# Channel-major and token-major operands, four 64x64 array tiles and 768-column weight blocks in an attention, MoE and MLP kernel

## The chip, the core and the metric

The kernel runs on one core of a Trainium2 chip. Five engines work side by side, each through its own queue in order: PE (the matmul array; PEld is its weight load), DVE (VectorE), ACT (ScalarE), POOL (GpSimd) and SP, which here issues DMAs. SBUF is the working memory, PSUM holds what PE writes. The metric is the device time of one execution in microseconds (us); lower is better.

## What is computed

A decayed linear attention over 768 tokens, then a mixture of four relu experts, then one MLP with h*cos(h):

```python
# attention: B, H, S, D = 4, 8, 768, 48
for t in range(S):
    cur = np.einsum('bhd,bhe->bhde', u[None] * kt, vt)
    y[:, :, t] = np.einsum('bhd,bhde->bhe', rt, state + cur)
    state = w[None, :, :, None] * state + np.einsum('bhd,bhe->bhde', kt, vt)
# x is y as (3072, 384); mixture: E, F = 4, 1024
for e in range(E):
    out += p[:, e:e + 1] * (np.maximum(x @ w1[e], 0.0) @ w2[e])
# MLP: d_ff = 2048
h = x @ w_in
return (h * np.cos(h)) @ w_out
```

## The kernel before

**Attention.** The tokens are cut into 24 cells, each of 128 tokens of one batch (two chunks `ch` of 64) with all eight heads, in four pairs `p` of an even and an odd head (`par`). A cell goes through these steps. `a_load` brings r, k and v as [128 tokens, 8 heads, 48]. `a_prep` (POOL) multiplies r and k with powers of the decay (`wr_tok`, `wk_tok`) and k with `u`. `a_tr` and `a_tk` turn r and k round on PE, four 128x128 transposes each (L203), and ACT copies them out of PSUM to `me`, `mo` (r of even and odd heads) and `kt`. `a_diag` and `a_bonus` make the diagonal term `dv` (DVE L181, L185, POOL L195). `a_score` multiplies k by r (L231), and DVE masks the result into the free halves of `me` and `mo` (L239). `a_state` multiplies k by v (L255), ACT copies the running state `st` beside v in `sv` (L266), and DVE moves `st` on by a chunk (L275, L276). `a_out` multiplies `me`, `mo` by `sv` (L289), DVE adds `dv` (L297). `a_x` turns the result round (L308) and splits it into `xh` and `xl`, a high and a low part, by ACT and DVE (`split`, L126, L127).

Every attention matmul (fp32) stands in the trace as two weight loads and two matmuls. Scores and state use the array as two tiles of 64 rows by 64 columns, one for the even and one for the odd head: rows 0 to 63 with columns 64 to 127, and rows 64 to 127 with columns 0 to 63. The outputs use two tiles of 128 rows by 64 columns.

**Mixture and MLP.** The work is a list of items (pass, unit, token block `j` of 512 tokens, block `q` of 128 hidden columns). A pass is half of the tokens, three token blocks; a unit is four blocks `q`. An item has nine matmuls up (L451 to L453) and, two or three items later, nine or twelve down (L506 to L508, L533 to L535). ACT and DVE make `gh` and `gl` between them (L460, L461), DVE and POOL add the expert's output to `acc` (L517, L520, L521). Weights of the mixture come as two staged tiles of [128, 384] per block `q` and are split into high and low by ACT and DVE (L126, L127); those of the MLP are decoded once, written to DRAM and read back by POOL's queue.

**Order.** It is written out by hand. A list `lead` opens the program with the first cells; then every item of the loop takes attention steps from a sorted list, by `offsets`, and `mix` puts them between the item's groups of three matmuls. In unit 0 of pass 0 the token blocks are cut into halves of 256 columns, and an item of a half needs `xh` and `xl` of its two cells: the six halves ask for cells 0 and 1, 2 and 3, and so on. The other twelve cells, for the second pass, are spread over the units that follow, up to item `N_ATT`. Attention's PSUM tiles come from `bank`: six banks in the opening, then a ring of three. Each of the six steps on PE takes one bank.

## Time and profile before

| | us |
|---|---|
| median of 3 runs (1336.24 to 1337.51) | 1336.41 |
| the profiled execution | 1336.83 |
| its span, first to last instruction | 1335.1 |
| opening, up to the first item's matmul | 25.7 |
| unit 0 of pass 0 | 110.2 |
| from there to the last attention step, with the other cells | 294.1 |
| all that follows | 905.1 |

The stretches are read from the starts of items' first matmuls, 25.7 and 135.9 us, and from the last attention step, shortly before 430 us. A row of the timeline gives start, length, engine, line, operation and tiles. Matmuls overlap, so what one costs is the time from its start to the start of the next, not its length. A row of the stretches gives busy time with the count of instructions for each engine, then the granted clock of PE, the share of the DMA engines and GB/s.

### The profile page before, as it was taken

The page shows a single profiled execution, that of the slowest core. Times are in us where ns is not written, and L with a number is a line of the kernel's source. Part 1 is how long each engine was busy: PE and PEld are TensorE (multiplying, and loading weights), DVE is VectorE, ACT ScalarE, POOL GpSimd, SP SyncE. Part 2 cuts the span into 40 slices and gives each one's busy share as a digit, 9 for nine tenths or more (in the row PEclk, how much of TensorE's full clock was granted, in tenths as well). Part 3 has the DMA queues.
Part 4 walks back from the last instruction along what each step waited for, and adds up shares of the span by engine and source line. Part 5 has one row for each costly group of instructions (what it writes and reads, how often), then busy time and mean ns, then how long its engine had stood idle before and what let it go on. Part 6 is the DMA issues. An engine that isn't in the chain of part 4 may idle for free.

```text
span 1335.1 us, 21064 instructions
## 1 busy us (share of the span) xinstructions
PE 1316.1 (99%) x8221; PEld 1127.2 (84%) x8221; DVE 850.5 (64%) x1490; ACT 594.7 (45%) x1158; POOL 294.8 (22%) x304
## 2 busy tenths in 40 slices
PE   8999999999999999999999999999999999999997
PEld 5898888888888888888888888888899999999997
DVE  7666546445444457667577577644877778777776
ACT  5775433433441122222221122214666667766664
POOL 5433233333312222102222222222111011011000
PEclk9999999999999999999999999999999999999999
DMA  8533332232112334433433334114122024122012
GB/s 171 115 69 74 76 92 71 62 82 64 44 58 58 110 110 145 147 97 115 121 110 120 102 111 134 63 56 145 60 83 83 24 83 131 48 84 83 24 37 73
DMA packets 166093, 118.14 MB, mean 88 GB/s; under 512 B 81409, under 2 KB 149730, under 8 KB 165986
## 3 DMA queue, kind: packets, MB, share of 16 engines
q1 hardware_dynamic: 156770, 91.55, 24.2%
q0 software_dynamic: 9216, 25.17, 6.4%
q8 instruction: 67, 1.10, 0.3%
q14 instruction: 40, 0.33, 0.1%
HBM read 94.62 MB, written 22.07 MB: 87 GB/s over the span
## 4 chain that ended last, share of the span: by engine, by line
PE 92%; DVE 3%; ACT 2%; issue 1%; DMA 1%; POOL 0%; SPq 0%; DVEq 0%; ACTq 0%; POOLq 0%
PE hp L451 15%; PE hp L452 14%; PE hp L453 14%; PE a L506 10%; PE a L508 9%; PE a L507 9%; PE a L533 4%; PE a L535 4%; PE a L534 4%; PE bank L289 2%; PE bank L231 2%; PE bank L203 1%; PE m L535 1%; PE m L534 1%; PE m L533 1%
## 5 line engine op out<-in xcount | busy, mean ns | idle before, releaser
L451 PE MATMUL hp<-xh,w 128*128 128x512 f32 (+1 forms) x900 | 350.3, 389 | 3.3 <-ACT xh L126 3.3
L452 PE MATMUL hp<-xl,w 128*128 128x512 f32 (+1 forms) x900 | 345.0, 383 | 0.7 <-DVE xl L127 0.7
L453 PE MATMUL hp<-xh,w 128*128 128x512 f32 (+1 forms) x900 | 344.9, 383 | 0.0
L460 ACT ACTIVATE gh<-hp 128x512 fp32r<-128x512 f32 (+1 forms) x204 | 116.8, 573 | 454.5 <-PE hp L453 449.8
L461 DVE SCALAR_TENSOR_TENSOR gl<-hp,gh 128x512 fp32r<-128x512 f32 (+1 forms) x204 | 134.0, 657 | 275.2 <-ACT gh L460 275.2
L521 POOL TENSOR_TENSOR acc<-acc,pm 128x512 f32<-128x512 f32 x126 | 164.9, 1337 | 575.5 <-DVE pm L520 575.5
L506 PE MATMUL a<-gh,w 128*128 128x512 f32 (+1 forms) x612 | 233.4, 381 | 0.4 <-DVE pm L520 0.4
L508 PE MATMUL a<-gl,w 128*128 128x512 f32 (+1 forms) x612 | 230.5, 377 | 0.0
L507 PE MATMUL a<-gh,w 128*128 128x512 f32 (+1 forms) x612 | 230.4, 376 | 0.0
L451 PEld LDWEIGHTS hp<-xh,w 128*128 128x128 f32 x900 | 169.4, 188 | 33.7 <-ACT xh L126 4.2
L453 PEld LDWEIGHTS hp<-xh,w 128*128 128x128 f32 x900 | 169.2, 188 | 33.0
L452 PEld LDWEIGHTS hp<-xl,w 128*128 128x128 f32 x900 | 169.5, 188 | 29.8 <-DVE xl L127 1.3
L506 PEld LDWEIGHTS a<-gh,w 128*128 128x128 f32 x612 | 115.0, 188 | 22.7 <-DVE pm L520 0.8
L507 PEld LDWEIGHTS a<-gh,w 128*128 128x128 f32 x612 | 115.1, 188 | 21.2
L508 PEld LDWEIGHTS a<-gl,w 128*128 128x128 f32 x612 | 115.0, 188 | 21.3
L520 DVE TENSOR_TENSOR pm<-a,pb 128x512 f32<-128x512 f32 x126 | 82.7, 684 | 33.8 <-POOL acc L521 33.8
L374 POOL DMA_DIRECT2D w<-dec x64 | 34.1, 536 | 315.6 <-PE m L535 158.5
L480 DVE SCALAR_TENSOR_TENSOR hs<-rr,hs 128x512 f32<-128x512 f32 x96 | 67.3, 701 | 52.4 <-ACT rr L479 52.4
L533 PE MATMUL a<-w,gh 128*128 128x384 f32 x288 | 97.4, 338 | 0.7 <-DVE acc L542 0.5
L478 ACT ACTIVATE rr<-rr 128x512 f32<-128x512 f32 x96 | 60.8, 633 | 82.6 <-DVE rr L473 82.6
L535 PE MATMUL a<-w,gl 128*128 128x384 f32 x288 | 97.4, 338 | 0.0
L534 PE MATMUL a<-w,gh 128*128 128x384 f32 x288 | 96.9, 336 | 0.0
(129 smaller groups left out, 1856.5 us busy)
## 6 DMA issues: line engine op xcount, KB each, us to landing
s<-in_moe_w_dram SPq DMA_DIRECT2D x128, 192.0 KB, 2.7
w<-dec POOLq DMA_DIRECT2D x64, 384.0 KB, 3.4
pb<-pn SPq DMA_DIRECT2D x48, 256.0 KB, 4.1
dec<-dout SPq DMA_DIRECT2D x32, 384.0 KB, 2.6
draw<-in_moe_w_in_dram SPq DMA_DIRECT2D x16, 384.0 KB, 4.2
draw<-in_moe_w_out_dram SPq DMA_DIRECT2D x16, 384.0 KB, 3.6
ldv<-in_v_dram SPq DMA_DIRECT2D x24, 192.0 KB, 3.3
out_dram<-acc SPq DMA_DIRECT2D x24, 192.0 KB, 2.4
```

The source lines that it names most:

```text
L451: nc.tensor.matmul(hp, wh[:, kk, :], x_h[:, kk, :], start=kk == 0, stop=False)
L452: nc.tensor.matmul(hp, wh[:, kk, :], x_l[:, kk, :], start=False, stop=False)
L453: nc.tensor.matmul(hp, wl[:, kk, :], x_h[:, kk, :], start=False, stop=kk == KD - 1)
L460: nc.scalar.activation(out=gh, in_=hp, func=ACTF.Relu)
L461: nc.vector.scalar_tensor_tensor(out=gl, in0=hp, scalar=0.0, in1=gh.bitcast(F32), op0=ALU.max, op1=ALU.subtract)
L506: nc.tensor.matmul(a, wh[:, ds], gh, start=q == 0, stop=False)
L507: nc.tensor.matmul(a, wl[:, ds], gh, start=False, stop=False)
L508: nc.tensor.matmul(a, wh[:, ds], gl, start=False, stop=q == BLK - 1)
L521: nc.gpsimd.tensor_tensor(out=o, in0=o, in1=m, op=ALU.add)
L533: nc.tensor.matmul(a, gh[:, ts], wh, start=q == 0, stop=False)
L534: nc.tensor.matmul(a, gh[:, ts], wl, start=False, stop=False)
L535: nc.tensor.matmul(a, gl[:, ts], wh, start=False, stop=q == BLK - 1)
```

## The change

The inputs are laid out anew: `rkt` holds r and k of a cell with channels on the partitions (48 of 64, for even heads above, for odd heads below), `rkv` holds r, k and v of a cell with tokens on the partitions, `vs` holds v as `sv` wants it, and `moe_wb`, `moe2_wb` hold both halves of a weight block in 768 columns. The steps `a_tr`, `a_tk`, `a_prep` and `a_fill` go. DVE multiplies r with the decay (`a_r`) and the token-major k (`a_kp`), POOL the channel-major k (`a_kt`). Scores and state put the two chunks into different tiles, so that four tiles of 64x64 are named in turn, with a bank for each chunk. `a_os` joins a cell's output with the next cell's score, `a_sx` a cell's state with an earlier cell's `a_x`.

```diff
-    def a_load(c, names="rkv"):
+    def a_load_t(c):
+        t = ld_p.tile([128, 2, HP, 128], F32, tag="rkt", name="rkt")
+        for o in (0, 64):
+            nc.sync.dma_start(out=t[o:o + 64], in_=rkt[b, i, o:o + 64])
+    def a_load_tok(c):
+        t = ld_p.tile([128, 3, H, D], F32, tag="rkv", name="rkv", bufs=4)
+        nc.sync.dma_start(out=t.rearrange("q x h d -> q (x h d)"), in_=rkv[b, i])
+    def a_load_v(c):
+        for hb in range(2):
+            nc.sync.dma_start(
+                out=sv[c % NSV][64 * hb:64 * hb + 64, 1 - hb].rearrange("q c p d -> q (c p d)"),
+                in_=vs[b, i, 64 * hb:64 * hb + 64],
+            )
...
+    def a_r(c):
+        m2 = t_p.tile([128, 2, HP, 128], F32, tag="m2", name="m2")
         for par in range(2):
+            x = slice(64 * par, 64 * par + 64)
+            nc.vector.tensor_tensor(
+                out=m2[x, par], in0=ld[c]["t"][x, 0], in1=tr[x].rearrange("q p c t -> q p (c t)"), op=ALU.mult
+            )
+    def a_kt(c, eng=None):
+        t = ld[c]["t"][:, 1]
+        (eng or nc.gpsimd).tensor_tensor(out=t, in0=t, in1=tk.rearrange("q p c t -> q p (c t)"), op=ALU.mult)
+    def a_kp(c, eng=None):
+        t = ld[c]["tok"][:, 1]
+        (eng or nc.vector).tensor_tensor(out=t, in0=t, in1=wk_tok[:, :, 0:D], op=ALU.mult)
...
     def a_diag(c):
-        a_rku(c)
+        a_rk(c)
         a_sum(c)
+        a_kp(c)
...
-        sc = bank([128, HP, 2, C], "sc")
+        sc = [bank([128, HP, C], "sc") for _ in range(2)]
         for p in range(HP):
             for ch in range(2):
                 for par in range(2):
-                    x0, a0 = 64 * par, 64 * (1 - par)
+                    x0 = 64 * par
+                    a0 = 64 * (1 - par) if ch == 0 else x0
                     nc.tensor.matmul(
-                        sc[a0:a0 + 64, p, ch, :],
+                        sc[ch][a0:a0 + 64, p, :],
...
+    def a_mask(c):
+        for ch in range(2):
+            for par in range(2):
+                o = 64 * (1 - par)
+                a0 = o if ch == 0 else 64 * par
+                nc.vector.tensor_tensor(
+                    out=d["m2"][o:o + 64, par, :, ch * C:ch * C + C],
+                    in0=sc[ch][a0:a0 + 64],
+                    in1=mask[a0:a0 + 64].unsqueeze(1).to_broadcast([64, HP, C]),
+                    op=ALU.mult,
+                )
...
-        up = bank([128, 2, HP, D], "ub")
+        up = [bank([128, HP, D], "ub") for _ in range(nch)]
+        for p in range(HP):
+            for ch in range(nch):
                 for par in range(2):
-                    x0, a0 = 64 * par, 64 * (1 - par)
+                    x0, h, a0 = 64 * par, 2 * p + par, 64 * ch
+                    k0 = (H + h) * D
                     nc.tensor.matmul(
-                        up[x0:x0 + 64, ch, p, :],
-                        (kp_[a0:a0 + 64, 2 * p + par, :] if ch != par else klp_[a0:a0 + 64, p, :]),
-                        s_[a0:a0 + 64, ch, p, par, :],
+                        up[ch][x0:x0 + 64, p, :], flat[a0:a0 + 64, k0:k0 + 64], tok[a0:a0 + 64, 2, h, :],
                         start=True, stop=True,
                     )
...
-    def a_pair(c):
-        a_score(c)
-        a_state(c)
+    def a_os(c):
+        if c > 0:
+            a_out(c - 1)
+        if c < NC_:
+            a_score(c)
+    def a_sx(c):
+        if c < NC_:
+            a_state(c)
+        if c - 2 in ld:
+            a_x(c - 2)
...
-        t = wp_.tile([128, 2, DM], F32R, tag=f"w{half}", name="w")
+        t = wp_.tile([128, 2, 2 * DM], F32R, tag="w", name="w")
         if un < NU1:
-            src = staged.pop(key)
-            split(t[:, 0], t[:, 1], src.rearrange("p k f -> p (k f)") if half == 0 else src)
+            split(t[:, 0], t[:, 1], staged.pop(key))
         else:
-            nc.gpsimd.dma_start(out=t, in_=dec[un, q, half].bitcast(F32R))
+            nc.gpsimd.dma_start(out=t, in_=dec[un, q].bitcast(F32R))
```

Two places show how instructions move. The first is PE at the end of unit 0, between the groups of three matmuls of the items. Before, these blocks of a cell stand there (transposes of r, output, transposes of k, score, state):

```order
L203 MATMUL bank<-ident,rp_115 128x128 x4
L506 MATMUL a_1469<-gh,w 128x256
L507 MATMUL a_1469<-gh,w 128x256
L508 MATMUL a_1469<-gl,w 128x256
...
L289 MATMUL bank<-sv_123,me 64x48 x2
L289 MATMUL bank<-sv_123,mo 64x48 x2
...
L203 MATMUL bank<-ident,kp_119 128x128 x4
...
L231 MATMUL bank<-me,kt 64x64
L231 MATMUL bank<-mo,kt 64x64
...
L255 MATMUL bank<-sv_122,klp_120 64x48
L255 MATMUL bank<-sv_122,kp_118 64x48
```

After the change a cell has two visits to PE, here in unit 1:

```order
L449 MATMUL hp<-xh_105,w 128x512
L282 MATMUL bank<-sv_116,m_1708 64x48 x16
L214 MATMUL bank<-m_1823,rkt 64x64 x16
L447 MATMUL hp<-xh_105,w 128x512
...
L449 MATMUL hp<-xh_105,w 128x512
L253 MATMUL bank<-rkv 64x48 x16
L447 MATMUL hp<-xh_105,w 128x512
```

The transposes have left; output and score stand in one piece, and so do state and, for the first twelve cells, `a_x`. The second place is DVE in unit 0, from one cell's `xl` to the next cell's. Before:

```order
L127 TENSOR_TENSOR xl_109<-bank,xh_106 128x3x128
L461 SCALAR_TENSOR_TENSOR gl<-hp,gh 128x256
L181 TENSOR_TENSOR rku<-rku,ldr 128x384
L185 TENSOR_REDUCE dsum<-rku 128x8
L297 TENSOR_TENSOR yo<-bank,dv 128x384
L461 SCALAR_TENSOR_TENSOR gl<-hp,gh 128x256
L239 TENSOR_TENSOR me<-bank,mask 64x512
L239 TENSOR_TENSOR mo<-bank,mask 64x512
L275 TENSOR_TENSOR stt<-bank,st_125 128x192
L276 TENSOR_TENSOR st_125<-stt,w_105 128x192
```

After:

```order
L128 TENSOR_TENSOR xl_109<-bank,xh_106 128x3x128
L181 TENSOR_TENSOR rkv<-rkv 128x384
L185 TENSOR_REDUCE dsum<-rkv 128x8
L190 TENSOR_TENSOR rkv<-rkv,wk_tok 128x384
L457 SCALAR_TENSOR_TENSOR gl<-hp,gh 128x256 x2
L290 TENSOR_TENSOR yo<-bank,rkv 128x384
L228 TENSOR_TENSOR m_963<-bank,mask 64x4x64 x4
L167 TENSOR_TENSOR m_1132<-rkt,tr 64x512 x2
L457 SCALAR_TENSOR_TENSOR gl<-hp,gh 128x256
L270 TENSOR_TENSOR stt<-bank,st_119 128x192
L271 TENSOR_TENSOR st_119<-stt,w_104 128x192
```

Two mask instructions have become four of half the size, and three multiplications (L190 once, L167 twice) have come to DVE from POOL and from ACT's copies.

## Rows read from the trace of the kernel before

**Rows 1.** The page's busy times: us, share of the span, count.

```profile
PE 1316.1 (99%) x8221; PEld 1127.2 (84%) x8221; DVE 850.5 (64%) x1490; ACT 594.7 (45%) x1158; POOL 294.8 (22%) x304
```

**Rows 2.** Stretches: opening with half 1, halves 3, 4 and 6, the later stretch.

```profile
0.00:50.50 50.50, 41.83 (x588) 32.66 (x588) 37.04 (x79) 31.95 (x76) 26.83 (x42) 0.97 0.65 137
...
68.90:86.90 18.00, 18.00 (x288) 17.21 (x287) 12.11 (x29) 12.77 (x32) 7.47 (x8) 1.00 0.34 67
86.90:107.30 20.40, 18.22 (x289) 17.22 (x287) 15.12 (x32) 14.11 (x36) 7.79 (x8) 1.00 0.39 90
...
127.20:135.90 8.70, 8.70 (x75) 8.70 (x74) 4.47 (x12) 2.61 (x7) 0.18 (x1) 1.00 0.03 8
135.90:430.00 294.10, 294.10 (x2204) 242.35 (x2204) 145.08 (x240) 113.50 (x245) 92.69 (x80) 1.00 0.26 68
```

**Rows 3.** DVE's and PE's timelines late in half 4 of unit 0.

```profile
100.84 2.59 DVE L127 TENSOR_TENSOR w<-s,w 128x384 fp32r<-128x384 f32 x2 [0.55 <-ACT w L126]
...
107.26 0.38 PE L451 MATMUL hp<-xh,w 128*128 128x256 f32 x1 [2.18 <-ACT xh L126]
```

**Rows 4.** PE's timeline around one cell's four transposes of r.

```profile
258.67 0.39 PE L453 MATMUL hp<-xh,w 128*128 128x512 f32 x1
258.90 0.60 PE L203 MATMUL bank<-ident,rp 128*128 128x128 f32 x4
...
259.58 0.39 PE L452 MATMUL hp<-xl,w 128*128 128x512 f32 x1
```

**Rows 5.** PE's timeline around one output, 32 matmuls in eight such rows.

```profile
263.21 0.39 PE L453 MATMUL hp<-xh,w 128*128 128x512 f32 x1
...
263.68 0.29 PE L289 MATMUL bank<-sv,mo 128*64 128x48 f32 x4
...
264.38 0.29 PE L289 MATMUL bank<-sv,mo 128*64 128x48 f32 x4
...
264.93 0.39 PE L452 MATMUL hp<-xl,w 128*128 128x512 f32 x1
```

**Rows 6.** PE's timeline around one score and state, 64 such matmuls.

```profile
273.13 0.39 PE L453 MATMUL hp<-xh,w 128*128 128x512 f32 x1
...
273.62 0.22 PE L231 MATMUL bank<-me,kt 64*64 64x64 f32 x1
273.62 0.22 PE L231 MATMUL bank<-mo,kt 64*64 64x64 f32 x1
...
275.79 0.39 PE L452 MATMUL hp<-xl,w 128*128 128x512 f32 x1
```

**Rows 7.** Groups on PE from 135.9 to 430 us: count, busy us, mean ns, idle.

```profile
L231 PE MATMUL bank<-me,kt 64*64 64x64 f32 x176 | 12.6, 221 | 0.0
...
L255 PE MATMUL bank<-sv,kp 64*64 64x48 f32 x144 | 10.1, 217 | 0.0
...
L203 PE MATMUL bank<-ident,rp 128*128 128x128 f32 x44 | 6.6, 272 | 0.0
```

**Rows 8.** DVE's timeline in half 3 of unit 0.

```profile
69.23 0.55 DVE L181 TENSOR_TENSOR rku<-rku,ldr 128x384 f32<-128x384 f32 x1
...
74.48 0.69 DVE L239 TENSOR_TENSOR me<-bank,mask 64x512 f32<-64x512 f32 x1
...
77.42 0.36 DVE L276 TENSOR_TENSOR st<-stt,w 128x192 f32<-128x192 f32 x1 [0.42 <-ACT sv L266]
...
80.91 0.41 DVE L517 TENSOR_TENSOR acc<-a,pb 128x256 f32<-128x256 f32 x1
```

**Rows 9.** POOL's and DVE's timelines where both run, after unit 0.

```profile
183.90 4.11 POOL L521 TENSOR_TENSOR acc<-acc,pm 128x512 f32<-128x512 f32 x3 [12.17 <-DVE pm L520]
185.82 1.02 DVE L181 TENSOR_TENSOR rku<-rku,ldr 128x384 f32<-128x384 f32 x1
```

**Rows 10.** DVE's timeline, its first work on data.

```profile
3.79 0.17 DVE L630 TENSOR_SCALAR wpair<-wpair 128x4 f32<-128x4 f32 x1 [2.48 <-DMA wpair<-in_w_dram]
```

**Rows 11.** A group on DVE before 50.5 us, columns as in rows 7.

```profile
L276 DVE TENSOR_TENSOR st<-stt,w 128x192 f32<-128x192 f32 x6 | 2.8, 468 | 2.3 <-ACT sv L266 2.2
```

## The prediction

> **What bounds the kernel now.** I read the page's busy times first: PE is busy for 99% of the span, no other engine for more than 64% [rows 1]. That is a mean over unlike stretches, so the table of stretches comes next [rows 2]. From 135.9 to 430 us PE is busy without a gap; what attention takes off PE there comes off the time. In halves 3 and 6 of unit 0 it is the same, 18.00 of 18.00 and 8.70 of 8.70 us. The difference, 9.30 us, is the price of two cells on PE. Before 50.5 us PE is short by 8.7 us, while DVE is busy for 37.0. In half 3 DVE has 12.11 of 18.00 us. So DVE could become the bound where cells are wanted quickly. Its lateness already shows once: two weight splits of 2.59 us hold it up, and soon after PE waits 2.18 us for `xh` [rows 3].

> **PE: what a cell costs before.** Two neighbouring 512-column matmuls start 0.227 us apart (258.67 to 258.90, rounded [rows 4]). From the matmul before a block to the second one after it, less two such steps, is the block's price with all change of array shape. Transposes: 259.58 - 258.67 - 0.45 = 0.45 us [rows 4], twice a cell. Output: 264.93 - 263.21 - 0.45 = 1.27 [rows 5]. Score and state: 275.79 - 273.13 - 0.45 = 2.20 [rows 6]. That is 4.37 us a cell; `a_x` has the 0.28 left of half the 9.30.

> **PE: what a cell costs after.** The two tiles in use run side by side: even and odd head start together [rows 6]. In the output, whose two tiles share all rows, 24 matmuls start in 264.38 - 263.68 = 0.70 us [rows 5], so a pair takes 0.058 and 16 pairs 0.93 us. Twice that is 1.86 in score and state too, for the rest of a block is the same in both: 2.20 - 1.86 = 0.34 and 1.27 - 0.93 = 0.34, the way to the smaller shape and back. The new code names four tiles in turn. No row shows four at once. If each tile keeps its pace of 0.058, a score takes 0.46 us; if only two run, 0.93. I take 0.46, since the pace is the same whether the two tiles share rows or not. Output with score then costs 0.34 + 0.93 + 0.46 and the change of shape between them, which no row shows: from 0 to another 0.34; I take 0.10, a third, as one of the three turns that a visit then has. That is 1.83 us. State costs 0.34 + 0.46 = 0.80, with `a_x` 1.08. A cell costs 2.63 us, or 2.91 with `a_x`, against 4.37 and 4.65.

> [...]

> **From 135.9 to 430 us.** The groups on PE [rows 7] have 44 transposes of r, 11 blocks of four, and those of k one block fewer: 21; twice 176 score matmuls, 11 scores of 32; twice 144 state matmuls, 7 states of 32 and 4 of 16; and there are 12 outputs. Before: 21 x 0.446 + 12 x 1.27 + 7 x 2.20 + 4 x (2.20 - 16 x 0.029) = 46.9 us. After: 11 outputs with score, one output alone and 10 states: 20.1 + 1.3 + 8.0 = 29.4. The last four states use two tiles, 0.46 for half the work. PE bounds this stretch and DVE is busy for 145 of 294 us in it [rows 2], so **17.5 us** go. Bounds: 18.6 with a free change of shape, 9.6 with two tiles only.

> **Unit 0: DVE.** Per cell DVE loses two masks of 0.69 and gets four of half the size, 0.41 by the nearest form, `acc` from PSUM [rows 8]: +0.26. `a_r` adds two multiplications of 64x512, 0.69 each as the mask: +1.38. `a_kp` adds one of 128x384, 0.55 as L181 [rows 8]: +0.55. Together 2.2 us a cell, 4.4 a half: 12.1 becomes 16.5 us. DVE also waits 0.42 us a cell for ACT's copies of the state [rows 8], which stay: 17.3. And `a_kp` stands right behind the sum that releases POOL's `dv`. Where POOL runs, L181 takes 1.02 instead of 0.55 us [rows 8, 9]. With 0.47 a cell more a half takes 18.3 us. PE needs 8.7 + 2 x 2.91 = 14.5. So DVE sets the pace, and the 3.5 us a half that PE saves are not seen.

> Before, halves 2 to 5 take 127.2 - 50.5 = 76.7 us, among them weight splits on DVE worth 15.1 - 12.1 = 3.0 [rows 2] and the stall. After, 4 x 18.3 + 3.0 = 76.2: -0.5. Half 6 has no attention: 8.7 again.

> Opening and half 1: DVE was busy for 37.0 of 50.5 us. Its new order up to `xl` of cell 3 gains twelve `a_r` (8.3 us), two `a_kt` (1.4), three L181 and one sum that POOL did or that are a cell ahead (2.2), six `a_kp` (3.3), one more cell's state (1.5) and masks (1.4); it loses six multiplications of the old opening and a `gl` (4.5): +13.6, to 50.6. Its start, 3.8 us with the wait for the decay [rows 10], and 2.2 us of waits for ACT [rows 11] can't be filled: half 2 starts at about 56.5 instead of 50.5, **+6 us**. The lock on six `a_kp` (+2.8) I set against starts of independent instructions that overlap a little.

> Unit 0 thus ends 5.5 us later, with bounds of -4 (no lock, starts overlap) and +20 (a later rival).

> **What costs nothing.** ACT loses four copies of r and k and, but for the first cells, those of v; it was never the bound [rows 1]. POOL has three operations a cell instead of four, and was busy for 7.5 of 18 us. A cell's DMA grows from 0.6 to 1.3 MB, in long runs: 145 GB/s at a cell each 9 us, where the opening moved 137 GB/s at a DMA share of 0.65 with runs of 192 bytes [rows 2]. SP's queue holds loads behind a load that waits for an old tile; a weight block is asked for three blocks ahead, which hides this. A wide weight block keeps its place until its down matmuls are done; the next use is two items away, 8 us. Without these covers PE would wait at each unit's start, some 3 us.

> **Sum.** The profiled execution took 1336.8 us, its span 1335.1; the median of the runs is 1336.4. I sum against the first: 1336.8 + 5.5 - 17.5 = 1324.8, **1325 us**.

> **Rivals.** *Only two tiles at once.* Unit 0 keeps its pace (PE needs 16.4 a half), the later stretch saves 9.6: 1336.8 + 5.5 - 9.6 = 1333. For it: no row shows four.

> *DVE is lighter than summed.* `a_kp` never meets POOL and independent starts overlap: unit 0 ends 4 us earlier, 1336.8 - 4 - 17.5 = 1315.

> *POOL blocks DVE wherever it can.* `a_r` and the splits meet POOL too: +0.47 on 12 `a_r` before half 2 (5.6), on 16 in the four halves (7.5), and +1 for splits: 1325 + 14 = 1339. The two splits of 2.59 us are such [rows 3]; against it, masks and sums from PSUM stand between, and POOL is idle for over half of a half [rows 2]. [...]

> *The bank ring (slower).* A visit now takes all three banks of the ring: output and two scores, then two states and `a_x`. PE can't begin a visit before DVE has read the last one, and if DVE has nothing else to do meanwhile, both take turns: a half grows by up to 2 x (1.83 + 1.08) = 5.8 us, four halves by 23: 1325 + 23 = 1348. It decides from about 3.5 us a half. Against it: `a_r` and `gl`, then `a_kp`'s group, about 1.8 us each, stand between DVE's last read and its next need.

> **How the numbers follow.** The forecast gets 0.48 (1318 to 1333), two tiles 0.18, the lighter DVE 0.12, the lock 0.10, the ring 0.12. A measurement of this kernel can tell about 0.2%, 2.7 us, from no change. Faster (under 1333.7): 0.47 + 0.10 + 0.12 + 0.02 = 0.71; same: 0.01 + 0.08 + 0.05 + 0.01 = 0.15; slower: 0.14. The range of 8 in 10 reaches from below the lighter DVE to past the lock: 1312 to 1341.

> **What would show it.** Right: a score whose four tiles start together and which lasts near 0.5 us; halves 2 to 5 near 18 us with PE waiting and DVE nearly full; half 2 starting near 56 us; the stretch up to the last attention step some 17 us shorter. Wrong: a half of 15 us (PE still sets it) or of over 20; a score that lasts 0.9; `a_kp` at 0.55 all along; or a change after 430 us, where I expect none.

## The result, and the profile after

The changed kernel takes 1346.8 us (median; 1345.6 to 1348.5, but for one execution of 1622.0 us in a slow state) against 1336.4 for the kernel before. The ratio is 1.0078, 95% interval 1.0063 to 1.0094: slower by about 10 us, where 1325 was forecast. The profiled execution took 1346.82 us, its span 1345.1. The busy times, to be held against [rows 1]:

```profile
PE 1291.3 (96%) x8025; PEld 1100.3 (82%) x8025; DVE 887.6 (66%) x1543; ACT 499.1 (37%) x888; POOL 271.1 (20%) x249
```

PE does 25 us less work, and the run still ends 10 us later, so PE now stands idle. Where, the table of stretches says. The engines stand in it in the order PE, PE's weight loads, DVE, ACT, POOL. The cuts are the first up matmul of the same items as in [rows 2]: opening with half 1, halves 2 and 3, half 6, then the 60 items from unit 1 on, which hold the rest of the attention in both kernels.

```profile
0.00:70.60 70.60, 41.90 (x572) 31.81 (x572) 51.39 (x110) 17.60 (x40) 23.40 (x37) 0.66 0.63 171
70.60:91.40 20.80, 16.89 (x271) 15.31 (x271) 16.94 (x38) 5.29 (x14) 6.57 (x7) 0.92 0.71 198
91.40:112.30 20.90, 16.82 (x270) 15.29 (x270) 16.82 (x38) 5.19 (x14) 6.45 (x7) 0.92 0.50 127
154.70:163.40 8.70, 8.70 (x72) 8.70 (x73) 3.93 (x10) 2.00 (x5) 3.20 (x4) 1.00 0.01 2
163.40:437.20 273.80, 273.80 (x2074) 223.63 (x2073) 155.85 (x261) 65.49 (x121) 87.00 (x68) 1.00 0.33 92
```

Half 2 starts at 70.6 instead of 50.5: +20.1. Halves 2 to 5 take 84.1 instead of 76.7: +7.4. Half 6 is 8.70 as before. The 60 items from unit 1 on are 273.8 (they took 290.8 before): -17.0. From there to the last item's start it is 890.0 instead of 890.7. The sum is +9.8, close to the 10.0 between the two spans.

The section on the time before puts the last attention step shortly before 430 us. It comes earlier: DVE adds the last output from 405.5 us on in the kernel before and from 283.1 on in the changed one. The rows are DVE's timelines of the kernel before and of the changed one, then the changed kernel's stretch from unit 1 to the item behind that step.

```profile
405.50 0.55 DVE L297 TENSOR_TENSOR yo<-bank,dv 128x384 f32<-128x384 f32 x1
```

```profile
283.08 0.55 DVE L290 TENSOR_TENSOR yo<-bank,rkv 128x384 f32<-128x384 f32 x1
```

```profile
163.40:286.30 122.90, 122.90 (x1409) 98.61 (x1408) 100.47 (x184) 33.69 (x71) 50.77 (x41) 1.00 0.54 146
```

The 60 items are full on PE. The four tiles do run at once, as PE's timeline of unit 1 shows, once cut off at 207.30 us and once whole: of a score, 12 matmuls start in the 0.2 us before 207.30, and 32 are done in 0.69.

```profile
207.09 0.40 PE L214 MATMUL bank<-m,rkt 64*64 64x64 f32 x12
207.09 0.69 PE L214 MATMUL bank<-m,rkt 64*64 64x64 f32 x32
```

In the opening, the largest wait stands on three engines at once. These are the timelines of SP, ACT, DVE and PE, in this order (start, duration, operation; in brackets the idle time before and what ended it):

```profile
33.41 1.79 SPq L138 DMA_DIRECT2D rkt<-in_rkt_dram  x2
44.75 1.10 SPq L150 DMA_DIRECT2D sv<-in_vs_dram  x2
45.96 0.53 SPq L144 DMA_DIRECT2D rkv<-in_rkv_dram  x1
46.59 1.10 SPq L138 DMA_DIRECT2D rkt<-in_rkt_dram  x2
47.78 0.54 SPq L357 DMA_DIRECT2D s<-in_moe_wb_dram  x1
```

```profile
55.51 0.84 ACT L127 ACTIVATE w<-s 128x768 fp32r<-128x768 f32 x1 [8.38 <-DMA s<-in_moe_wb_dram]
```

```profile
56.38 0.96 DVE L128 TENSOR_TENSOR w<-s,w 128x768 fp32r<-128x768 f32 x1 [6.74 <-ACT w L127]
```

```profile
57.67 1.95 PE L282 MATMUL bank<-sv,m 128*64 128x48 f32 x32 [8.50 <-DVE stt L270]
```

SP issues nothing from 35.2 to 44.75: the load of `sv` waits for an old tile, which PE's output still has to read. The load of the fourth weight block stands behind it and behind 1.3 MB of loads of one cell. ACT and DVE have its split next in their order, so both stop, and with them the steps of the state that stand behind the split: PE's output waits for the first of them on DVE (L270). SP's waits up to 80 us (in all, times, longest) name both holds of the opening; the one at hand is 9.5 us of the 31.1, the longest, 11.3, comes after the weight block has been issued:

```profile
SPq L150 <- PE bank L282: 31.1, 4, 11.3
SPq L663 <- DVE p_out L660: 10.0, 1, 10.0
```

In half 3 PE and DVE wait for each other. DVE's timeline first, then PE's:

```profile
90.88 0.75 DVE L457 SCALAR_TENSOR_TENSOR gl<-hp,gh 128x256 fp32r<-128x256 f32 x2
93.41 0.56 DVE L290 TENSOR_TENSOR yo<-bank,rkv 128x384 f32<-128x384 f32 x1 [1.78 <-PE bank L282]
94.46 1.75 DVE L228 TENSOR_TENSOR m<-bank,mask 64x256 f32<-64x256 f32 x4 [0.49 <-PE bank L214]
```

```profile
91.35 0.38 PE L447 MATMUL hp<-xh,w 128*128 128x256 f32 x1 [1.56 <-DVE gl L457]
91.90 1.47 PE L282 MATMUL bank<-sv,m 128*64 128x48 f32 x32
93.30 1.13 PE L214 MATMUL bank<-m,rkt 64*64 64x64 f32 x32
```

PE needs `gl`, which frees an up bank, and `gl` stands behind the 1.65 us of `a_diag` on DVE. When it is done, DVE's next work is the output's copy, and PE has only just begun the up matmuls ahead of that output.

### The profile page after: what moved, and what is told of

It is laid out like the page before. It is cut to its first block, busy times and chain, and to the rows that moved or that the text cites. A ratio compares the mean times of both kernels' runs of the same rounds, so it can differ in the third digit from the quotient of the medians.

```text
span 1345.1 us, 20223 instructions
## 1 busy us (share of the span) xinstructions
PE 1291.3 (96%) x8025; PEld 1100.3 (82%) x8025; DVE 887.6 (66%) x1543; ACT 499.1 (37%) x888; POOL 271.1 (20%) x249
## 3 DMA queue, kind: packets, MB, share of 16 engines
q1 hardware_dynamic: 66834, 108.46, 27.2%
## 4 chain that ended last, share of the span: by engine, by line
PE 88%; DVE 5%; issue 2%; DMA 2%; ACT 1%; SPq 1%; POOL 0%; DVEq 0%; POOLq 0%; ACTq 0%
PE hp L447 15%; PE hp L448 14%; PE hp L449 14%; PE a L504 9%; PE a L502 9%; PE a L503 9%; PE a L529 4%; PE a L531 4%; PE a L530 4%; DMA rkt<-in_rkt_dram 1%; PE bank L282 1%; PE m L531 1%; PE m L530 1%; PE m L529 1%; DVE m L228 1%
## 5 line engine op out<-in xcount | busy, mean ns | idle before, releaser
L517 POOL TENSOR_TENSOR acc<-acc,pm 128x512 f32<-128x512 f32 x126 | 169.6, 1374 | 549.7 <-DVE pm L516 549.7
L468 DVE SCALAR_TENSOR_TENSOR rr<-ni,hs 128x512 f32<-128x512 int32 x96 | 66.3, 691 | 42.6 <-ACT ni L467 42.6
```

Source lines behind the costliest of these rows:

```text
L517: nc.gpsimd.tensor_tensor(out=o, in0=o, in1=m, op=ALU.add)
```

## The experiments

The lock is the name in the prediction and in the expectations for a longer time of a DVE product beside POOL's: in the changed kernel a pair of L167 took 1.88 us beside POOL and 1.41 alone.

**The weight block asked for early.** The theory: the order on SP costs the 6.7 us.

```
 lead_w = {..., (a_out, 1): (3, 1)}
+        # one entry more: (a_x, 0): (4, 1)
```

> The load of the fourth weight block stands ahead of the loads of cells 3 to 6 on SP's queue; nothing else changes. Theory (order on SP): in the changed kernel this load stood behind a load of v that waits for an old tile until PE has done an output, was issued at 47.8 us and landed 7.7 us later, so ACT waits 8.4 and DVE 6.7 us. With the load early this wait goes: half 2 starts near 64 instead of 70.6 us and the run takes near 1340 us. Rival (traffic: the cells' loads are twice as large, 1.3 MB each): the block then pushes the cells' loads back by as much, half 2 starts within 2 us of 70.6, and the run stays at 1345 to 1348. Rival (clock: TensorE at half its clock in the opening): the wait goes, but half 2 starts no earlier than 68.

Measured: 1340.4 us, ratio to before 1.003 (1.002 to 1.0039); half 2 starts at 64.1. The split now finds its block (ACT's timeline, no wait in brackets):

```profile
47.44 0.85 ACT L127 ACTIVATE w<-s 128x768 fp32r<-128x768 f32 x1
```

6.4 of the 10 us were one load's place in a queue; the traffic itself did not push back.

**`a_diag` behind `gl`.** Each `a_os(c)` calls `a_diag(c + 1)` first, instead of the planner placing it before.

```
     def a_os(c):
+        if 3 <= c < NC_ - 1:
+            a_diag(c + 1)
         if c > 0:
```

> On DVE the product r k, its sum and the product of k with its table (1.65 us a cell) stand right ahead of the cell's output copy instead of ahead of the two low halves gl that free the up banks. Theory (the two engines take turns through their orders): PE no longer waits 1.56 us a half for gl, and DVE no longer stands 1.8 us a half before the output; halves 2 to 5 take 19.2 to 19.8 us instead of 20.3 to 22.1, and the run takes 1340 to 1343 us. Rival (DVE's instructions alone set the half, with the lock against POOL): halves stay within 0.4 us and the run within 2 us of 1346.8. Rival (the three banks of the ring decide): PE's wait moves from gl to the score's bank, halves stay.

Measured: 1349.2 us, 1.0093 (1.0076 to 1.0111). The halves did what the first theory said: 18.8, 19.1, 21.3, 19.1, together 78.3 instead of 84.1. But the 60 items from unit 1 on lost 9.0 us: they take 282.8, of which PE stands still for 5.0, and it waits there for DVE, as it never did before the edit; the granted clock over these items was 0.99 instead of 1.00. A row of the table of stretches for half 3, and one of PE's timeline in unit 1:

```profile
88.20:107.30 19.10, 15.47 (x271) 13.92 (x271) 17.23 (x38) 5.21 (x14) 6.55 (x6) 1.00 0.53 141
```

```profile
267.09 0.67 PE L253 MATMUL bank<-rkv 64*64 64x48 f32 x16 [2.22 <-DVE yo L290]
```

The mechanism was right; the forecast of the total was wrong, since I forgot that the same order also rules the stretch in which PE is full.

**Two tiles at a time.** The loops of score and state put the chunk outermost.

```
-        for p in range(HP):
-            for ch in range(2):
+        for ch in range(2):
+            for p in range(HP):
```

> The loops of score and state run over the chunk outermost, so neighbouring matmuls name only two of the four array tiles. Theory (four tiles run at once only if neighbours name four): a score of 32 lasts 0.93 instead of 0.48 us, a state too; the stretch from unit 1 to the last attention step takes 17 x 0.46 = 7.8 us longer (281.6 instead of 273.8), unit 0 up to 0.9 us a half longer where DVE waits for the output and score behind it: 1355 to 1359 us. [...]

Measured: 1352.4 us, 1.0116 (1.0099 to 1.0133). The 60 items from unit 1 on take 278.7, +4.9, which lies between no loss at all and the theory's 7.8. Reckoned as in the prediction, output with score costs 2.18 instead of 1.89 us and a state 1.08 instead of 0.81, so +0.29 and +0.27 where 0.46 was expected. A score lasts (PE's timeline):

```profile
198.97 0.97 PE L214 MATMUL bank<-m,rkt 64*64 64x64 f32 x32
```

The order of names matters, 0.97 us against 0.69 for a score, but the second pair of tiles begins before the first has ended: in this trace at 0.29 us into a score.

**The clock.** Four idle matmuls ahead of each score, state and output of the opening.

```
-    WARM_AT = {a_x: 2, a_out: 1}
+    WARM_AT = {a_x: 2, a_out: 4, a_score: 4, a_state: 4}
```

> Four idle 512-column matmuls ahead of each score, state and output of the opening (one ahead of an output before), so that TensorE is busy while it waits. Theory (order): the clock rises in the opening, but DVE's instructions and the late weight block set its length: half 2 starts within 2 us of 70.6, the run takes 1345 to 1349 us. Rival (clock): the opening at half clock is what costs the time; half 2 starts 5 us earlier or more, 1342 us or less.

Measured: 1347.9 us, 1.0088 (1.0071 to 1.0104); half 2 starts at 70.4.

```profile
0.00:36.60 36.60, 23.26 (x313) 12.70 (x314) 28.72 (x63) 8.97 (x20) 14.04 (x28) 0.90 0.85 217
```

The clock rose from 0.69 to 0.90 up to the first item, and that item starts 0.5 us later. So up to there the clock is not what the opening waits for. From the first item to half 2 the clock was 0.66 against 0.63, so for that part this run tells nothing. In halves 2 and 3, which had 1.00 here, 20.3 and 20.2 us stand against 20.8 and 21.0 at 0.92: some 0.6 us a half.

**Both gains together.** The early block, and `a_diag` late for cells 4 to 11 alone.

> Both single changes that gained time in unit 0: the early load of the fourth weight block (it gave 6.4 us) and, for cells 4 to 11 alone, the product, its sum and the table product behind gl (for all cells it shortened unit 0 by 7.0 us and lengthened unit 1 by 9.0). Theory (the two losses are independent, and the loss in unit 1 came from the late order there): half 2 starts near 63, halves 2 to 5 take 78 to 79 us, from the start of unit 1 to the first item after the last attention step it is 273.8 again; 1346.8 - 6.4 - 6.0 = 1334 us, bounds 1332 to 1337. Rival (the same DVE time is counted twice): 1338 to 1341.

Measured: 1337.1 us, 0.9998 (0.9988 to 1.0007). The 60 items from unit 1 on are back at 273.8. Halves 2 and 3 take 19.1 each, but 4 and 5 22.8 and 21.9: their cells are already 12 to 14. With `range(4, 15)` in place of `range(4, 12)`:

> As the kernel with both changes, with the late place of the three DVE operations for cells 4 to 14 instead of 4 to 11, since the last two halves of unit 0, whose cells are 12 to 14, kept their 22.8 and 21.9 us. Theory (gl behind these operations costs there too): halves 4 and 5 fall to 21.3 and 19.1 us as where it held for all cells, 4.3 us less: 1337.0 - 4.3 = 1332.7 us, bounds 1331 to 1335, faster than the kernel before. Rival (the late order costs as much in unit 1, where these cells' states are used): 1336 to 1338.

Measured: 1334.2 us, 0.9979 (0.997 to 0.9989); halves 19.1, 19.1, 21.3, 19.1, the 60 items 274.1. The two losses add, and they were 12.6 us together.

**The table product of k on POOL**, with both gains (cells 4 to 11).

```
-        a_kp(c)
+        a_kp(c, nc.gpsimd if c in LATE else None)
```

> As the kernel with both changes, and besides the table product of k for cells 4 to 11 is done by POOL, between its products with u and with the sum. Theory (DVE's instructions now set the half, 17 of 19 us): DVE loses 1.1 us a half, halves 2 to 5 take some 4 us less in all, 1330 us, bounds 1328 to 1333. Rival (lock): POOL works 2 us more a half beside DVE, whose multiplications with two SBUF inputs grow from 0.55 or 0.69 to over 1 us, and nothing is gained: 1333 to 1337. Rival (chain): POOL's later product with the sum makes the output late, 1336 or more.

Measured: 1336.5 us, 0.9997 (0.9988 to 1.0007), not told apart from the kernel with both gains. Half 3 stays at 19.1, though DVE lost two instructions of 0.55. This is DVE's `a_r` in half 3 (count, busy, mean ns):

```profile
L167 DVE TENSOR_TENSOR m<-rkt,tr 64x512 f32<-64x512 f32 x4 | 4.1, 1026 | 0.1
```

In the kernel with both gains the four took 3.6 us there. So 0.5 of the 1.1 us went back into `a_r`, which now meets more of POOL's work (8.43 us of it in the half, 6.55 in the kernel with both gains). Most of the other 0.6 went into a wait for PE's output that the kernel with both gains does not have at this place (DVE's timeline, half 3):

```profile
83.15 0.56 DVE L290 TENSOR_TENSOR yo<-bank,rkv 128x384 f32<-128x384 f32 x1 [0.41 <-PE bank L282]
```

**The other hold on SP.** The store of the normalized weights goes to POOL's queue; nothing else is changed.

```
-        nc.sync.dma_start(out=pn.rearrange(...), in_=p_out)
+        nc.gpsimd.dma_start(out=pn.rearrange(...), in_=p_out)
```

> The changed kernel, with the store of the normalized weights, for which SP's queue stands 10.0 us in the opening, moved to POOL's queue. Theory (of the holds on SP only the one ahead of the fourth weight block costs, since that load stays behind the load of v that waits for PE's output): half 2 starts within 1 us of 70.6 and the run takes 1345 to 1348 us. Rival (every hold on SP costs, as the loads are twice as large): half 2 starts 4 us earlier or more, 1343 us or less.

Measured: 1350.3 us, 1.0102 (1.0085 to 1.0119). The first item starts at 39.1 instead of 36.1. Half 2 starts at 73.2, so theory and rival both missed. The wait only changed its queue: POOL now stands before it, and its next three products run in one piece. One of DVE's two products for cell 2, 0.69 us alone, started while POOL was at the store and took 4.58, until 0.56 us behind the third of them. These are POOL's, DVE's and PE's timelines:

```profile
24.98 0.87 POOL L663 DMA_DIRECT2D pn<-p_out  x1 [6.27 <-DMA rkv<-in_rkv_dram]
25.88 1.27 POOL L173 TENSOR_TENSOR rkt<-rkt,tk 128x512 f32<-128x512 f32 x1
27.11 0.99 POOL L177 TENSOR_TENSOR rkv<-rkv,u_tok 128x384 f32<-128x384 f32 x1
28.06 1.25 POOL L173 TENSOR_TENSOR rkt<-rkt,tk 128x512 f32<-128x512 f32 x1
```

```profile
25.29 4.58 DVE L167 TENSOR_TENSOR m<-rkt,tr 64x512 f32<-64x512 f32 x1
```

```profile
29.93 1.13 PE L214 MATMUL bank<-m,rkt 64*64 64x64 f32 x30 [2.25 <-DVE m L167]
```

PE's score waits for that product; in the changed kernel the product ends at 26.9, here at 29.9, and the first item comes 3.0 us later too. POOL's late products with k are not the cost, as the score begins at 27.2 in this run and at 27.3 in the changed kernel. Nor did SP come free: its load of `pb` waits for the store and goes at 30.64 instead of 30.88 us, and the next loads behind it 0.4 us earlier. Only the loads that stand ahead of that one came earlier, by 7 to 10 us.

```profile
30.64 0.39 SPq L668 DMA_DIRECT2D pb<-pn  x1
```

So whether this hold on SP costs anything is not decided by this run. What was missed is who stands behind the wait in its new place.

**The weight blocks alone**, put into the kernel before, with its loads and splits counted in blocks.

> The kernel before with one part of the change alone: weights in 768-column blocks, loaded and split by block. Theory (this part costs nothing where no load ahead of it waits for PE): 1334 to 1339 us, half 2 within 1 us of 50.5. Rival (the wide block itself holds ACT and DVE up in unit 0, or lands late): half 2 starts 3 us later or more, 1340 us or more.

Measured: 1335.3 us, 0.9987 (0.9978 to 0.9997); half 2 starts at 50.6. The wide block is harmless in the kernel before, where nothing ahead of its load waits for PE.

**One product of r per cell.** On top of the version with cells 4 to 14, `a_r` multiplies in place over 128 rows, the score reads it there, and ACT copies the halves.

```
-        for par in range(2):
-            x = slice(64 * par, 64 * par + 64)
-            nc.vector.tensor_tensor(out=m2[x, par], in0=ld[c]["t"][x, 0], in1=tr[x]..., op=ALU.mult)
+        nc.vector.tensor_tensor(out=t, in0=t, in1=tr..., op=ALU.mult)
...
+            nc.scalar.activation(out=d["m2"][x, par], in_=d["t"][x, 0], func=ACTF.Copy)
```

> As the former, and r is multiplied by its decay once per cell in place, one DVE instruction of 128 x 512 instead of two of 64 x 512; the score reads it there, and ACT copies both halves to the tile that the output reads. DVE loses 0.69 us a cell, ACT gets two copies of about 0.59. Theory (DVE's instructions set unit 0, its order being mended): halves 2 to 5 take 1.4 us less each, half 2 starts 3 to 5 us earlier (eight cells before it, not all binding): 1332.7 - 5.6 - 4 = 1323 us, bounds 1319 to 1328. Rival (what is left is taking turns with PE, as the table product on POOL took 0.4 to 1.1 us from DVE and the halves stayed at 19.1): halves within 0.4 us, 1330 to 1334. Rival (ACT's copies make gh or the state's copies late): 1333 or more.

Measured: 1325.6 us, 0.9917 (0.99 to 0.9933): faster than both kernels. Half 2 starts at 59.7; the halves take 17.7, 17.7, 19.8, 17.7. DVE is busy for 15.89 of the 17.7 us of half 3; with cells 4 to 14 alone it was 17.23 of 19.1 (first row):

```profile
81.30:100.40 19.10, 15.48 (x271) 13.93 (x271) 17.23 (x38) 5.21 (x14) 6.56 (x6) 1.00 0.52 140
```

```profile
77.40:95.10 17.70, 15.53 (x271) 14.00 (x271) 15.89 (x36) 7.72 (x19) 6.56 (x6) 1.00 0.60 158
```

DVE's busy time fell by 1.34 us and the half by 1.4. So with the order mended, DVE's instructions set halves 2 to 5, as the prediction had it.

## Why the prediction was wrong

**PE's cells: right.** Output with score 1.89 us (1.83 forecast), state 0.81 (0.80), the stretch -17.0 (-17.5). Half 6 and the time behind the stretch hardly changed (890.0 against 890.7). One reason given for the stretch did not hold: that DVE is busy for 145 of 294 us in it. The loop gives each item at least one of the attention's blocks on PE, and there are 22 of them now instead of 44, so the attention of the second pass ends after 23 items instead of 55, and in these DVE is busy for 100.5 of 122.9 us. PE stayed full with less room than counted; `a_diag` behind `gl` for all cells used it up. The rival of two tiles at once is refuted, and its price was too high: naming two at a time adds 0.28, not 0.46, a block. Two of the four tiles share each half of the rows, and still 12 matmuls of a score start within 0.2 us.

**Halves 2 to 5: the step "so DVE sets the pace" failed.** DVE's busy time was well summed: 16.8 us, with 17.4 forecast. Added to it were only ACT's copies. Missing were DVE's waits for PE: 1.5 to 1.8 us for the output in every half and 0.5 for the score in halves 2 and 3. The rows of the order ahead of the prediction already show it: L181, L185, L190, then `gl` twice, then L290. An engine's sum is a pace only if nothing in its order waits for the engine that waits for it. I had the taking of turns as a rival, but at the ring of three banks, and dismissed it because other DVE work stood between; that work stood ahead of `gl`, on the wrong side. Moving `a_diag` gave 5.8 of the 7.9 us by which the halves missed. Some of the 5.8 may be the clock: between the two kernels with the early block, whose clocks are alike (0.980 and 0.983 over the run), the halves differ by 4.6 (83.3 and 78.7). The rest of the 7.9 is open. The rival's 1348 us is close to the measured time by luck: its mechanism is another, and more than half of the miss lies in another stretch.

**Opening: DVE's sum was right, its waits were not.** This is the larger miss, 14.1 of the 22 us between 1346.8 and the forecast (+20.1 against +6). Busy 51.4 us against 50.6; idle 19.2 against the 6.0 allowed. "SP's queue holds loads behind a load that waits for an old tile; a weight block is asked for three blocks ahead, which hides this" is the sentence that failed: three blocks are in hand at the start, the fourth is asked for after the waiting load, and its price was 6.4 us, where I had put some 3 as the loss without cover and not counted it. Of the rest, the trace shows DVE waiting 0.7, 1.2 and 1.2 us for three first states that PE can begin only after DVE's own L190, and 1.3 for POOL's first product. No run tested these, and the cause of this rest, 7.7 us, stays open.

**The lock: a term of the wrong size and place.** What is behind it no run shows; the times are these. L190 was charged 1.02 us and took 0.55 or 0.56 in 23 of 24 cells, though POOL's `dv` runs beside it in 17 of them; there it is POOL's instruction that takes 1.08 instead of 0.83. Only at 20.24 us it took 1.35. `a_r`, charged nothing, pays: 1.41 us a pair alone, 1.88 beside POOL. The rows are DVE's in the opening and in half 3, then POOL's.

```profile
20.24 1.35 DVE L190 TENSOR_TENSOR rkv<-rkv,wk_tok 128x384 f32<-128x384 f32 x1
96.24 1.41 DVE L167 TENSOR_TENSOR m<-rkt,tr 64x512 f32<-64x512 f32 x2
101.67 0.55 DVE L190 TENSOR_TENSOR rkv<-rkv,wk_tok 128x384 f32<-128x384 f32 x1
104.50 1.88 DVE L167 TENSOR_TENSOR m<-rkt,tr 64x512 f32<-64x512 f32 x2
```

```profile
20.06 1.11 POOL L177 TENSOR_TENSOR rkv<-rkv,u_tok 128x384 f32<-128x384 f32 x1
101.83 1.08 POOL L194 TENSOR_TENSOR rkv<-rkv,dsum 128x384 f32<-128x384 f32 x1 [8.00 <-DMA sv<-in_vs_dram]
104.12 0.98 POOL L177 TENSOR_TENSOR rkv<-rkv,u_tok 128x384 f32<-128x384 f32 x1
```

Which of them pays follows from the starts: the one that starts second. L190 starts 0.16 us before `dv` at 101.67 and 0.18 us behind POOL's product at 20.24. In the changed kernel it happens 23 times that a product of DVE (L167, L190) and one of POOL overlap by more than 0.1 us, each only with the other: the earlier of the two is at most 0.01 us longer than the shortest of its kind, the later is longer by 0.21 to 0.81.

**Costs nothing: partly right.** The wide blocks are free (1335.3 us alone), and the larger loads did not slow the early block (its split at 47.44 us had no wait). The queue order was not free.

## What to carry to other kernels

A load that waited for an old tile made everything behind it on SP's queue wait for PE, which frees that tile: 9.5 us in the opening, of which the run lost 6.4. Look what stands behind it, a weight block above all, and ask for that first. When work moves from the busiest engine to the next, don't stop at that engine's sum: follow its order and see whether an instruction that frees a bank stands behind work that could come later. An order that is right where one engine is the bound can be wrong in the next stretch: `a_diag` behind `gl` took 5.8 us off halves 2 to 5 and cost 9.0 from unit 1 on.

## What the runs showed of the hardware

```profile
L164 DVE TENSOR_TENSOR rkt<-rkt,tr 128x512 f32<-128x512 f32 x2 | 2.3, 1138 | 0.1
```

```profile
9.55 0.69 DVE L173 TENSOR_TENSOR rkt<-rkt,tk 128x512 f32<-128x512 f32 x1
```

In half 3 of the changed kernel the granted clock was 0.92: from 92.5 to 95.9 us it was 0.50, after PE had waited 1.56 us until 91.35, and up matmuls then started 0.21 instead of 0.12 us apart. In the kernel with the early block PE was busy for only 15.5 of 20.2 us in halves 2 and 3 and for 15.9 of 22.2 in half 4, and the clock stayed at 1.00. What decides between the two is open.
